# SyncE issues the copies of keys, and six of twelve first gathers are asked for later

## The chip, the core and the metric

The kernel runs on one core of a Trainium2 chip. The core has five engines that run side by side and wait for one another by semaphores: TensorE (PE, matmuls; its weight loads are shown apart as PEld), VectorE (DVE), ScalarE (ACT), GpSimd (POOL) and SyncE (SP, which computes nothing and issues transfers). ACT, SP and POOL can each issue a DMA transfer from their own queue; 16 DMA engines carry all of them. The metric is the device time of one execution in microseconds (us), lower is better.

## The reference

A token block of 2048 rows of 512 is normalised, and two layers are added to it: attention with 32 query heads of 16 and one shared key and value head, and a mixture of 4096 experts from which each token and head takes two, by two searches of 64 keys each.

```python
x = A_x
xn = _layernorm(x, axis=-1)
return x + _A_ref(xn, A_wq, A_wk, A_wv, A_wo) + _B_ref(xn, B_w_q, B_k1, B_k2, B_u, B_v)

# _A_ref: q = xn @ wq (32 heads of 16), k = xn @ wk, v = xn @ wv (one head)
p = softmax(q k^T * 16 ** -0.5);  out = (p v) @ wo
# _B_ref, for each token and head: the two best of 64 keys on either half of a query,
#   the two best of their four sums, gates g by a softmax over the two
act = gelu(xn . u[top_e]);  out = sum of g * act * v[top_e]
```

## The kernel before

Tokens stand in 16 tiles of 128, four tiles to a group, four groups. The program has two parts.

The start (lines 1179 to 1229) makes what attention needs, group by group. `norm_group` normalises four tiles (DVE, with one square root on ACT). `transpose_group` turns them on PE into `ptr` and splits each into a high and a low part `xt` or `xtt`, the high part by a cast on ACT (L181), the low one on DVE (L182); the later groups are stored to HBM (`dxt`, L185, four transfers of 512 KB). `project_kv` makes the keys and values of the group (`pkv`, L198), copies them out on ACT (`kv`, L201), splits them on DVE (`kh`) and then writes the 16 rows of keys six times into the tile `kaug`, which the attention scores read: L207, L208 and L209, once for each of two bases, 32 KB each. In the kernel before, ACT issues these six transfers. `project_q` makes the queries: four steps of 12 matmuls (`pq`, L227); each step is cast on ACT (`qt`, L231), its low part is made on DVE (L232), its square on ACT (`qsq`, L234) goes through one matmul on PE (`pqs`, L235), and SP stores both parts (`dqh`, `dql`, L237 and L238, 256 KB each). `qt` has four buffers, two for each step, so the third step's cast waits until the first step's stores have landed.

Between the second and the third group, the start also makes the expert search of the first chunk of heads: `pw` and `pwt` (L485, L492), 48 matmuls `psc` (L530), the two best by DVE (L543, L545) and from them row numbers. With these, twelve indirect gathers on POOL (L960, `g`, 512 KB each) fetch expert rows; `gathers(NGB)` in line 1217 asks for all twelve. The pool `g` has twelve buffers, so no further gather can start before the main part has used one.

At the end of the start `guard` (L251 to L265) reduces the largest norms to one flag; every engine reads it and branches.

The main part (from line 1230) is written out in a fixed order for all engines: attention in 512 steps (`sc` L325, exponential on ACT L328, `pv` L339), with the expert work laid in between.

The order of the start is made otherwise. A scheduler takes the instructions in the order of the code as a priority, weighs its own costs for each, and fixes for each engine a list that the engine then works off strictly in that order. So a change of the engine of one transfer can move instructions on all engines up to the flag, and none after it. The transfers that SP and ACT issue take eight semaphores (`DMAHW0` to `DMAHW7`) in turn; each issue waits until the transfer that had the same semaphore before, eight back, has landed. The gathers have eight of their own (`DMASW`).

Of the kernel before, what the change touches and what calls it, by code (L numbers as in the profile page):

```python
# [40 lines left out]
NGB = 12  # L41
# [14 lines left out]
def tile_kernel(ctx, tc, x, wq, wkv, wo, wqT, kT, uv, ub, vb, out):  # L56
    nc = tc.nc
# [11 lines left out]
    raw = lambda ap: ap.bitcast(F32)  # L69
# [23 lines left out]
    kaug = const.tile([P, S], F32R, name="kaug")  # L93
# [34 lines left out]
    def load_x(t, first):  # L128
        if first:
            xa = big.tile([P, 2, D], F32, name="xa", tag="xa", bufs=TPH)  # L130
            ACC[t], XN[t] = xa[:, 0, :], xa[:, 1, :]
            xs = xa[:, 0, :]
        else:
            if t % 2 == 0:
                if t // GT == 2:
                    XP[0] = big.tile([P, 2, D], F32, name="xp", tag="wk", bufs=NWK)
                else:
                    XP[0] = start.tile([P, 2, D], F32, name="xp", bufs=2)
            xs = XP[0][:, t % 2, :]
            XN[t] = xs  # L140
        nc.sync.dma_start(xs, x[t * P:(t + 1) * P, :])
        return xs
# [27 lines left out]
    def transpose_group(g):  # L170
        first = g < 1
        XT[g] = []
        for k in range(KC):
            if first:
                xt = big.tile([P, 2, 512], F32R, name="xt", tag="xt", bufs=4)
            else:
                xt = start.tile([P, 2, 512], F32R, name="xtt", tag="xtt", bufs=6)
            p = xtile("ptr")
            for j in range(GT):
                nc.tensor.transpose(p[:, j * P:(j + 1) * P], XN[g * GT + j][:, k * P:(k + 1) * P], ident)  # L180
            nc.scalar.copy(xt[:, 0, :], p)  # L181
            nc.vector.tensor_tensor(out=xt[:, 1, :], in0=p, in1=xt[:, 0, :], op=OP.subtract)  # L182
            XT[g].append(xt)
            if not first:
                nc.sync.dma_start(d_xt[g - 1][k], raw(xt[:]))  # L185
# [6 lines left out]
    def project_kv(g):  # L192
        p = stile("pkv")[:, 0, :]
        n = 0
        for k in range(KC):
            for a, b in TERMS:
                w = (wkv_h, wkv_l)[a]
                nc.tensor.matmul(p[:32, :], w[:, k, :], XT[g][k][:, b, :], start=n == 0, stop=n == 11)  # L198
                n += 1
        kv = big.tile([32, 512], F32, name="kv", tag="wk", bufs=NWK)  # L200
        nc.scalar.copy(kv, p[:32, :])  # L201
        kh = big.tile([32, 2, 512], F32R, name="kh", tag="wk", bufs=NWK)
        nc.vector.tensor_copy(kh[:, 0, :], kv)
        nc.vector.tensor_tensor(out=kh[:, 1, :], in0=kv, in1=kh[:, 0, :], op=OP.subtract)
        c = slice(g * 512, (g + 1) * 512)
        for base in (0, 64):
            nc.scalar.dma_start(raw(kaug[base:base + 16, c]), raw(kh[:16, 0, :]))  # L207
            nc.scalar.dma_start(raw(kaug[base + 16:base + 32, c]), raw(kh[:16, 1, :]))  # L208
            nc.scalar.dma_start(raw(kaug[base + 32:base + 48, c]), raw(kh[:16, 0, :]))  # L209
        sq = start.tile([16, 512], BF16, name="ksq", tag="sq", bufs=2)  # L210
        nc.vector.tensor_mul(sq, kv[:16, :], kv[:16, :])
        nc.tensor.matmul(ksq_p[32 * g:32 * g + 32, :], blk[:16, 0:1].to_broadcast([16, 32]), sq,
                         start=True, stop=True)
        pt = xtile("pv_t")
        for c in range(GT):
            nc.tensor.transpose(pt[:, 32 * c:32 * c + 32], kv[:, c * P:(c + 1) * P], ident[:32, :32])
        nc.vector.tensor_copy(vaug[:, GT * g:GT * g + GT, :DH],
                              pt[:, :P].rearrange("p (c n) -> p c n", n=32)[:, :, DH:])

    def project_q(g, wqs):  # L220
        pq = xtile("pqs")
        for r in range(KC):
            p = stile("pq")[:, 0, :]
            n = 0
            for k in range(KC):
                for a, b in TERMS:
                    nc.tensor.matmul(p, wqs[k][:, a, r * P:(r + 1) * P], XT[g][k][:, b, :],  # L227
                                     start=n == 0, stop=n == 11)
                    n += 1
            q = [start.tile([P, 512], F32R, name="qt", tag="qt", bufs=4) for _ in range(2)]  # L230
            nc.scalar.copy(q[0], p)  # L231
            nc.vector.tensor_tensor(out=q[1], in0=p, in1=q[0], op=OP.subtract)  # L232
            sq = start.tile([P, 512], BF16, name="qsq", tag="sq", bufs=2)
            nc.scalar.activation(sq, p, AF.Square)  # L234
            nc.tensor.matmul(pq[32 * r:32 * r + 32, :], blk, sq, start=True, stop=True)  # L235
            c = slice(g * 512, (g + 1) * 512)
            nc.sync.dma_start(d_qh[r * P:(r + 1) * P, c], raw(q[0][:]))  # L237
            nc.sync.dma_start(d_ql[r * P:(r + 1) * P, c], raw(q[1][:]))  # L238
        nc.vector.reduce_max(qmax[:, g:g + 1], pq, axis=AX.X)
# [713 lines left out]
    def gather(m):  # L953
        ph, c, ti, s = slots[m]
        if s == 0:
            run_scores(key=(ph, c, ti))
            if ph and c == 0:
                load_phase2_tile(TPH * ph + ti)
        gt = gtile()
        nc.gpsimd.indirect_dma_start(  # L960
            out=gt, out_offset=None, in_=uv,
            in_offset=bass.IndirectOffsetOnAxis(ap=IDX[ph, c, ti][:, s:s + 1], axis=0))
        UV[m] = gt
# [50 lines left out]
    def gathers(most):  # L1014
        while g_next[0] < NSL and g_next[0] < a_next[0] + NGB - lent[0] and most > 0:
            gather(g_next[0])
            g_next[0] += 1
            most -= 1
# [24 lines left out]
    def run(fns):  # L1043
        todo = fns[:]
        fns.clear()
        for fn in todo:
            fn()
# [147 lines left out]
    for i in range(2):  # L1195
        for k in range(2):
            w = start.tile([P, 2, 512], F32R, name="wqs", tag="wqs", bufs=4)
            nc.scalar.copy(w[:, 0, :], wraws[i][:, k, :])
            nc.gpsimd.tensor_tensor(out=w[:, 1, :], in0=wraws[i][:, k, :], in1=w[:, 0, :], op=OP.subtract)
            wqs.append(w)  # L1200
    project_kv(0)
    norm_group(1, xs[1])
    project_q(0, wqs)
    transpose_group(1)
    project_kv(1)
    for base in (48, 112):
        nc.scalar.dma_start(raw(kaug[base:base + 2, :]).rearrange("r (i n) -> r i n", n=512),
# [5 lines left out]
    project_q(1, wqs)  # L1213
    transpose_group(2)
    project_kv(2)
    xs.append([load_x(3 * GT + j, False) for j in range(GT)])
    gathers(NGB)
    project_q(2, wqs)
    norm_group(3, xs[3])
    transpose_group(3)  # L1220
    project_kv(3)
    project_q(3, wqs)
    run(STORES)
    start_stack.close()
# [90 lines left out]
def build(nc, tc, args):  # L1315
    tile_kernel(tc, *args)
# [33 lines left out]
```

## Time and profile before

| what | us |
|---|---|
| three runs, median (lowest, highest) | 1978.41 (1978.28, 1985.47) |
| profiled execution | 1969.9 |
| its span, first to last instruction | 1968.2 |
| PE busy | 1871.4 |
| DVE busy | 1678.5 |
| ACT busy | 1291.5 |
| POOL busy | 563.0 |
| the flag is written on DVE at | 131.2 |
| first matmul of attention (`sc`) at | 147.9 |

The start is the first 131 us of the span, the branch and the first weights take the next 16, and the rest is the main part. All times of single instructions below are counted from the start of the span. In a row of the timeline stand the start, the time from start to end of the whole row, the engine, the line, the operation and, in brackets, how long the engine was idle before it and what it waited for. `ACTq` and `SPq` are an engine's queue, which issues transfers.

### The profile page before, as it was taken

How to read it: one execution, taken by the hardware profiler on the slowest of the kernel's cores; microseconds unless marked ns; L12 is line 12 of the kernel's file. 1: busy time of each engine (PE TensorE's matmuls, PEld its weight loads, DVE VectorE, ACT ScalarE, POOL GpSimd, SP SyncE). 2: the span in 40 equal slices, each digit the busy share in tenths (PEclk: the TensorE clock that was granted, in tenths of full speed). 3: DMA queues.
4: the chain of work that ended last, by engine and by line, in shares of the span. 5: the costliest groups of instructions: out<-in, count | busy, mean ns of one | idle time of the engine just before them, and what ended most of it. 6: DMA issues, size and time to landing. Idle time of an engine off the chain costs nothing.

```text
span 1968.2 us, 34715 instructions
## 1 busy us (share of the span) xinstructions
PE 1871.4 (95%) x10990; PEld 993.5 (50%) x10990; DVE 1678.5 (85%) x6713; ACT 1291.5 (66%) x1801; POOL 563.0 (29%) x540
## 2 busy tenths in 40 slices
PE   6879999999998998999999999999989899999997
PEld 3544444555554543555555445555545454555552
DVE  6527888999998975899999789999989878899993
ACT  3326666655556885778777555655568877788773
POOL 2202223321222222344344232222222224343420
PEclk9989999999998899999999999999988899999998
DMA  7756879887764886798889987777647878788872
GB/s 281 280 198 232 294 264 304 288 294 240 252 216 137 215 233 213 236 289 290 266 290 312 345 291 255 266 264 236 205 130 210 255 230 285 246 295 267 270 250 80
DMA packets 238041, 492.16 MB, mean 250 GB/s; under 512 B 93204, under 2 KB 93204, under 8 KB 237852
## 3 DMA queue, kind: packets, MB, share of 16 engines
q0 software_dynamic: 73728, 268.47, 41.2%
q1 hardware_dynamic: 162120, 219.82, 34.1%
q10 hardware_dynamic: 2004, 1.61, 0.3%
q8 instruction: 88, 1.44, 0.3%
q14 instruction: 101, 0.83, 0.1%
HBM read 428.46 MB, written 56.07 MB: 246 GB/s over the span
## 4 chain that ended last, share of the span: by engine, by line
PE 65%; DVE 19%; DMA 5%; ACT 2%; issue 2%; SPq 0%; ACTq 0%; DVEq 0%
PE pv L339 19%; PE sc L325 13%; PE psc L530 9%; PE pout L846 9%; PE pact L722 9%; DVE i L545 5%; DVE m L543 3%; DVE xa L1007 3%; PE pg L804 3%; DVE g L972 3%; ACT pt L328 2%; PE pwo L432 2%; PE pw L485 1%; DMA dg<-gst 1%; DMA wqt<-in_wqT_dram 1%
## 5 line engine op out<-in xcount | busy, mean ns | idle before, releaser
L328 ACT ACTIVATE pt<-sc 128x1024 f32<-128x1024 f32 x1024 | 993.1, 1025 | 460.6 <-PE sc L325 459.5
L960 POOL DMA_INDIRECT g<-in_uv_dram,idx x512 | 550.1, 1074 | 1342.9 <-DVE xa L1007 703.0
L339 PE MATMUL pv<-pt,vaug 128*32 128x512 f32 x4096 | 517.1, 623 | 0.0
L325 PE MATMUL sc<-qa,kaug 64*128 64x512 f32 x2048 | 387.8, 454 | 21.0 <-ACT pt L328 20.6
L530 PE MATMUL psc<-wk,xt 128*128 128x512 f32 x1536 | 388.5, 400 | 2.4 <-DVE wk L495 2.0
L1007 DVE SCALAR_TENSOR_TENSOR xa<-g,w,xa 128x512 f32<-128x512 f32 x512 | 371.2, 744 | 0.0
L972 DVE CUSTOM_DVE_ANT_0 g<-g,xa 128x512 f32<-128x512 f32 x512 | 335.5, 680 | 1.0 <-DMA g<-in_uv_dram,idx 0.9
L530 PEld LDWEIGHTS psc<-wk,xt 128*128 128x128 f32 x1536 | 277.6, 188 | 106.1 <-issue 37.4
L325 PEld LDWEIGHTS sc<-qa,kaug 64*128 64x128 f32 x2048 | 156.8, 186 | 342.7 <-ACT pt L328 233.8
L339 PEld LDWEIGHTS pv<-pt,vaug 128*32 128x32 f32 x4096 | 109.8, 112 | 258.6 <-issue 257.0
L545 DVE FIND_INDEX8 i<-m,psc 128x8 uint32<-128x64 f32 x1024 | 206.3, 220 | 0.0
L846 PE MATMUL pout<-wk,wd 128*128 128x512 f32 x768 | 195.4, 402 | 2.8 <-DVE wd L904 2.7
L722 PE MATMUL pact<-xt,wk 128*128 128x512 f32 x768 | 195.9, 400 | 1.4 <-DVE i L545 1.4
L846 PEld LDWEIGHTS pout<-wk,wd 128*128 128x128 f32 x768 | 140.6, 188 | 50.8 <-DVE act L972 5.1
L722 PEld LDWEIGHTS pact<-xt,wk 128*128 128x128 f32 x768 | 139.4, 188 | 50.2 <-issue 17.9
L543 DVE MAX8 m<-psc 128x8 f32<-128x64 f32 x1024 | 145.9, 213 | 17.5 <-PE psc L530 16.8
L995 DVE SCALAR_TENSOR_TENSOR w<-gth,ga 128x4 f32<-128x4 f32 x128 | 20.2, 158 | 84.9 <-ACT gth L988 84.6
L687 DVE TENSOR_TENSOR wk<-rw,wk 128x512 fp32r<-128x512 f32 x128 | 85.0, 682 | 6.6 <-ACT wk L686 6.6
L849 DVE TENSOR_TENSOR da<-da,pout 128x512 f32<-128x512 f32 x128 | 82.8, 678 | 4.0 <-PE pout L846 3.6
L770 DVE TENSOR_TENSOR oh<-oh 128x2048 f16<-128x2048 f16 x64 | 78.0, 1218 | 0.0
L686 ACT CAST wk<-rw 128x512 fp32r<-128x512 f32 x128 | 73.9, 629 | 2.9 <-DMA rw<-in_ub_dram 2.9
L804 PEld LDWEIGHTS <-oh 128*128 128x128 f16 x1024 | 68.3, 165 | 14.4 <-issue 6.8
(155 smaller groups left out, 1337.2 us busy)
## 6 DMA issues: line engine op xcount, KB each, us to landing
wk<-dw SPq DMA_DIRECT2D x96, 512.0 KB
wqt<-in_wqT_dram SPq DMA_DIRECT2D x32, 512.0 KB
dw<-wk SPq DMA_DIRECT2D x32, 512.0 KB
rw<-in_ub_dram SPq DMA_DIRECT2D x64, 256.0 KB
rw<-in_vb_dram SPq DMA_DIRECT2D x64, 256.0 KB
gy<-dg SPq DMA_DIRECT2D x64, 256.0 KB
dg<-gst SPq DMA_DIRECT2D x30, 512.0 KB
qa<-dqh SPq DMA_DIRECT2D x128, 64.0 KB
```

The lines of the kernel that those rows point to most:

```text
L325: nc.tensor.matmul(p[:, b, :], kaug[o:o + 64, kc * P:(kc + 1) * P], QA[u][o:o + 64, i, :], start=True, stop=True)
L328: nc.scalar.activation(pt, p, AF.Exp, scale=SCALE)
L339: nc.tensor.matmul(PV[u][32 * j:32 * j + 32, :], vaug[:, kc, :], pt[:, b, :], start=kc == 0, stop=kc == 15)
L530: nc.tensor.matmul(p, XT[g][k][:, a, j * P:(j + 1) * P], WC[n_][k][:, bb, :], start=n == 0, stop=n == 11)
L543: nc.vector.max(m8[:, jb, s, :], p[:, s * E:(s + 1) * E])
L545: nc.vector.max_index(i8[:, jb, s, :], m8[:, jb, s, :], p[:, s * E:(s + 1) * E])
L722: nc.tensor.matmul(p, us[:, a, k * P:(k + 1) * P], XT[DG][k][:, c, :], start=n == 0, stop=n == 11)
L804: nc.tensor.matmul(p[:, i * NB:(i + 1) * NB], oa[:, :, i], ob[:, :, i], start=True, stop=True)
L846: nc.tensor.matmul(p, wd[0][:, a, j * P:(j + 1) * P], vs[:, c, :], start=n == 0, stop=n == 5)
L960: nc.gpsimd.indirect_dma_start(out=gt, out_offset=None, in_=uv, in_offset=bass.IndirectOffsetOnAxis(ap=IDX[ph, c, ti][:, s:s + 1], axis=0))
L972: nc.vector.tensor_tensor_reduce(u, u, XN[TPH * ph + ti], scale=1.0, scalar=0.0, op0=OP.mult, op1=OP.add, accum_out=a[:, i:i + 1])
L1007: nc.vector.scalar_tensor_tensor(acc, v, w[:, i:i + 1], acc, op0=OP.mult, op1=OP.add)
```

## The change

Two things are changed in the code. The six copies of keys of each group are issued by SP instead of ACT (24 transfers in all), and line 1217's twelve gathers are asked for in two halves: six where they stood, six after `project_kv(3)`, ahead of `project_q(3)`.

```diff
         for base in (0, 64):
-            nc.scalar.dma_start(raw(kaug[base:base + 16, c]), raw(kh[:16, 0, :]))
-            nc.scalar.dma_start(raw(kaug[base + 16:base + 32, c]), raw(kh[:16, 1, :]))
-            nc.scalar.dma_start(raw(kaug[base + 32:base + 48, c]), raw(kh[:16, 0, :]))
+            nc.sync.dma_start(raw(kaug[base:base + 16, c]), raw(kh[:16, 0, :]))
+            nc.sync.dma_start(raw(kaug[base + 16:base + 32, c]), raw(kh[:16, 1, :]))
+            nc.sync.dma_start(raw(kaug[base + 32:base + 48, c]), raw(kh[:16, 0, :]))
...
     xs.append([load_x(3 * GT + j, False) for j in range(GT)])
-    gathers(NGB)
+    gathers(NGB // 2)
     project_q(2, wqs)
     norm_group(3, xs[3])
     transpose_group(3)
     project_kv(3)
+    gathers(NGB // 2)
     project_q(3, wqs)
     run(STORES)
```

POOL's own list stays what it was: the twelve gathers follow each other, with nothing between them, ahead of the flag. What moves are the lists of PE, DVE, ACT and SP up to the flag. On PE, 73 of the `pq` matmuls stood ahead of the 48 `psc` matmuls, now 57: sixteen of the second group's queries go behind them.

The first place is ACT in the third group, from the last transposes to the queries. Before (in brackets the semaphores that each row waits for):

```order
L181 CAST xtt<-ptr 128x512 [waits DMAHW7_49,PE_49]
L201 COPY kv<-pkv 32x512 [waits PE_49]
L207 DMA kaug<-kh 16x512 [waits DMAHW0_49,DVE_49]
L209 DMA kaug<-kh 16x512 [waits DMAHW1_49]
L208 DMA kaug<-kh 16x512 [waits DMAHW2_49,DVE_49]
L207 DMA kaug<-kh 16x512 [waits DMAHW3_49]
L208 DMA kaug<-kh 16x512 [waits DMAHW4_49]
L209 DMA kaug<-kh 16x512 [waits DMAHW5_49]
L231 CAST qt<-pq 128x512 [waits PE_49,Activation_49] x2
L234 ACTIVATE qsq<-pq 128x512 [waits DVE_49] x2
```

The same place on ACT with the change:

```order
L181 CAST xtt<-ptr 128x512 [waits DMAHW2_49,PE_49]
L201 COPY kv<-pkv 32x512 [waits PE_49]
L231 CAST qt<-pq 128x512 [waits DMAHW3_49,PE_49,Activation_49]
L234 ACTIVATE qsq<-pq 128x512 [waits DVE_49]
L231 CAST qt<-pq 128x512 [waits DMAHW6_49,PE_49]
L234 ACTIVATE qsq<-pq 128x512 [waits DVE_49]
```

The six transfers are gone from ACT's list, and the queries' casts follow the keys at once.

The second place is SP in the same group, from the stores of the transposed tokens to the queries. Before:

```order
L185 DMA dxt_0_76<-xtt 128x1024 [waits DMAHW4_49,DVE_49]
L185 DMA dxt_1_77<-xtt 128x1024 [waits DMAHW5_49,DVE_49]
L185 DMA dxt_2_78<-xtt 128x1024 [waits DMAHW6_49,DVE_49]
L185 DMA dxt_3_79<-xtt 128x1024 [waits DMAHW7_49,DVE_49]
L237 DMA dqh<-qt 128x512 [waits DMAHW6_49,Activation_49]
L238 DMA dql<-qt 128x512 [waits DMAHW7_49,DVE_49]
```

The same place on SP with the change:

```order
L185 DMA dxt_0_76<-xtt 128x1024 [waits DMAHW0_49,DVE_49]
L185 DMA dxt_1_77<-xtt 128x1024 [waits DMAHW1_49,DVE_49]
L185 DMA dxt_2_78<-xtt 128x1024 [waits DMAHW2_49,DVE_49]
L185 DMA dxt_3_79<-xtt 128x1024 [waits DMAHW3_49,DVE_49]
L207 DMA kaug<-kh 16x512 [waits DMAHW4_49,DVE_49]
L208 DMA kaug<-kh 16x512 [waits DMAHW5_49,DVE_49]
L209 DMA kaug<-kh 16x512 [waits DMAHW6_49]
L207 DMA kaug<-kh 16x512 [waits DMAHW7_49]
L208 DMA kaug<-kh 16x512 [waits DMAHW0_49]
L209 DMA kaug<-kh 16x512 [waits DMAHW1_49]
L237 DMA dqh<-qt 128x512 [waits DMAHW2_49,Activation_49]
L238 DMA dql<-qt 128x512 [waits DMAHW3_49,DVE_49]
```

The six copies now stand between the stores of the tokens and those of the queries. The fifth and sixth copy wait for the first two `dxt` stores to land, the first step's `dqh` and `dql` for the last two.

The third place is ACT right behind the branch, at the first exponentials of attention. Before:

```order
L486 COPY wt<-pw 128x512 x4
L494 CAST wk<-pwt 128x512 x4
L328 ACTIVATE pt<-sc 128x1024 x8
L486 COPY wt<-pw 128x512
L328 ACTIVATE pt<-sc 128x1024 x2
```

With the change:

```order
L486 COPY wt<-pw 128x512 x4
L494 CAST wk<-pwt 128x512 x4
L328 ACT_TABLE_LOAD
L328 ACTIVATE pt<-sc 128x1024 x8
L486 COPY wt<-pw 128x512
L328 ACTIVATE pt<-sc 128x1024 x2
```

A load of ACT's function table has come in. The fourth group's square root (L153) now stands behind the expert search's exponential (L582) and no longer ahead of it, so it loads the table of the root, and the first exponential of attention loads that of the exponential again: two loads more than before.

## The prediction

> **What bounds the kernel now.** I read the page's busy times and its chain first, then the windows by stage, the waits of the start, and last the timeline there, because nothing behind the flag changes its order.
>
> ```profile
> PE 1871.4 (95%) x10990; PEld 993.5 (50%) x10990; DVE 1678.5 (85%) x6713; ACT 1291.5 (66%) x1801; POOL 563.0 (29%) x540
> PE 65%; DVE 19%; DMA 5%; ACT 2%; issue 2%; SPq 0%; ACTq 0%; DVEq 0%
> 0.00:131.24 131.24, 98.30 (x422) 64.37 (x422) 75.14 (x247) 40.41 (x72) 24.83 (x40) 0.96 0.74 267
> 131.24:160.00 28.76, 18.40 (x86) 6.77 (x90) 6.03 (x17) 13.24 (x18) 0.00 (x0) 0.81 0.55 182
> 160.00:1968.00 1808.00, 1754.74 (x10490) 922.40 (x10481) 1597.32 (x6449) 1237.81 (x1712) 538.17 (x500) 0.98 0.76 250
> ```
>
> The first two lines are the page's parts on busy time and on the chain; the windows give length, busy us of PE, PEld, DVE, ACT and POOL, the PE clock granted, the DMA share and GB/s. PE is the engine that paces the whole, 1754.7 of 1808 us in the main part. In the start it works 98.3 of 131.2 us. The main part is one fixed list per engine and waits for no clock time, so what the start gains or loses reaches the end one for one; I take that share as 1.
>
> Where PE stands in the start, the waits from 24 to 131 us say:
>
> ```profile
> PE pqs L235 <- ACT qsq L234: 14.2, 7, 6.3
> ACT qt L231 <- DMA kaug<-kh: 14.1, 2, 9.8
> ```
>
> PE waited 14.2 us in seven places for ACT's squares, once for 6.3 us; ACT in turn stood 14.1 us in two places behind the copies of keys. The timeline shows the copies on ACT's queue (first and last of the six of a group), what ACT did next, and PE beside it:
>
> ```profile
> 24.90 0.59 ACTq L207 DMA_DIRECT2D kaug<-kh  x1
> 28.56 0.94 ACTq L209 DMA_DIRECT2D kaug<-kh  x1
> 30.29 0.38 PE L235 MATMUL pqs<-qsq,blk 128*32 128x512 bf16 x1 [1.62 <-ACT qsq L234]
> 33.98 0.38 PE L235 MATMUL pqs<-qsq,blk 128*32 128x512 bf16 x1 [1.49 <-ACT qsq L234]
> 46.57 0.53 ACTq L207 DMA_DIRECT2D kaug<-kh  x1
> 50.05 0.53 ACTq L209 DMA_DIRECT2D kaug<-kh  x1
> 58.60 11.04 PE L530 MATMUL psc<-wk,xt 128*128 128x512 f32 x48
> 69.89 5.51 PE L227 MATMUL pq<-xtt,wqs 128*128 128x512 f32 x23
> 84.16 0.52 ACTq L207 DMA_DIRECT2D kaug<-kh  x1
> 91.53 1.83 ACTq L209 DMA_DIRECT2D kaug<-kh  x1
> 93.46 1.07 ACT L231 CAST qt<-pq 128x512 fp32r<-128x512 f32 x2 [9.77 <-DMA kaug<-kh]
> 95.45 0.59 PE L235 MATMUL pqs<-qsq,blk 128*32 128x512 bf16 x1 [6.28 <-ACT qsq L234]
> 112.31 0.52 ACTq L207 DMA_DIRECT2D kaug<-kh  x1
> 115.43 0.60 ACTq L209 DMA_DIRECT2D kaug<-kh  x1
> 119.00 0.38 PE L235 MATMUL pqs<-qsq,blk 128*32 128x512 bf16 x1 [1.23 <-ACT qsq L234]
> ```
>
> Six copies hold ACT's queue 4.6, 4.0, 9.2 and 3.7 us in the four groups. In the second group PE had other work; in the third nothing was left, and it stood 6.28 us. After that stall the clock was low:
>
> ```profile
> 94.00:96.00 2.00, 0.55 (x2) 0.04 (x1) 1.29 (x2) 1.72 (x4) 0.00 (x0) 0.54 1.02 391
> 96.00:98.00 2.00, 2.00 (x5) 0.92 (x5) 0.00 (x0) 0.00 (x0) 0.00 (x0) 0.50 1.04 367
> 98.00:100.00 2.00, 2.00 (x6) 1.52 (x6) 0.00 (x0) 0.00 (x0) 0.00 (x0) 0.50 1.04 418
> 100.00:102.00 2.00, 2.00 (x8) 1.64 (x7) 0.00 (x0) 0.17 (x1) 0.00 (x0) 0.75 1.01 404
> ```
>
> **The change, part by part.**
>
> *ACT loses the copies, third group.* The 6.28 us of idle time go. With them goes the slow clock behind: PE busy times what the clock lacked, 0.55 x 0.46 + 2 x 0.50 + 2 x 0.50 + 2 x 0.25, or 2.8 us by the four windows above. Together -9.1. The cover of this is DMA work, taken up below.
>
> *First and second group.* 1.62 + 1.49 = 3.1 us of idle PE hang on ACT's queue in the first group; in the second PE's idle time is nil. The new list puts sixteen transposes in a row on PE with four casts behind them on ACT, so part comes back. Ends 0 and -3.1; I take -2, nearer to the row that is removed.
>
> *Fourth group.* The 1.23 us at 119.00 are of the same kind, and the queue holds only 3.7 us there: -1.2, ends 0 and -1.2.
>
> *The gathers.* POOL's list is the same, so the second six go out right behind the first six as before: 0. They start when the search is ready, and that is earlier: sixteen `pq` matmuls (23 take 5.51 us, so 0.24 each) no longer stand ahead of the search, 3.8 us, and the 2 us above. The matmuls themselves are not saved.
>
> *SP gains the copies: the new wait.* The gathers fill the DMA engines:
>
> ```profile
> 74.63 1.11 POOL L960 DMA_INDIRECT g<-in_uv_dram,idx  x1 [59.24 <-DVE e L598]
> 78.64 3.89 SPq L185 DMA_DIRECT2D dxt<-xtt  x4
> 74.00:102.00 28.00, 20.27 (x82) 13.06 (x81) 10.60 (x34) 8.33 (x15) 11.90 (x12) 0.88 0.97 366
> q0 software_dynamic: 1710, 6.23, 59.4%
> q1 hardware_dynamic: 1507, 3.81, 34.6%
> g<-in_uv_dram,idx POOLq DMA_INDIRECT x12, 12.2
> ```
>
> From 74 to 102 us the DMA engines are 97% busy at 366 GB/s (the queue rows are of that window: packets, MB, share). A gather takes 12.2 us from issue to landing there, and SP issues four `dxt` stores in 3.9 us. In the new SP list the third group's first query stores stand behind four `dxt` stores and six copies, the last of which wait for two `dxt` to land, and `dql` for the fourth. The third step's cast on ACT needs those stores landed, and PE's next `pqs` needs that cast. By bytes: twelve gathers (6.3 MB), the second group's seven later stores (7 x 0.26), four `dxt` (2.1), copies and loads of 0.3 MB make 10.5 MB; at 390 GB/s, the middle of the fine windows, 27 us. The search began at 58.60 and the gathers 16.0 us later; now it begins near 53, the gathers near 69, and the stores land near 69 + 27 + 2 = 98 (2 us for the last store's own way, an estimate); cast, low part and square take 2.0 us, as from 93.46 to 95.45 above, so `pqs` can go near 100. PE's work from the search to that point is 11 us of `psc`, 87 `pq` at 0.24 (20.9), and some 8 us of 24 transposes, 12 `pkv` and small matmuls, with 2.7 us of short waits such as these of the third group:
>
> ```profile
> 77.25 0.41 PE L198 MATMUL pkv<-xtt,wkv_h 128*32 128x512 f32 x1 [0.50 <-ACT xtt L181]
> 78.62 0.38 PE L235 MATMUL pqs<-qsq,blk 128*32 128x512 bf16 x1 [0.95 <-ACT qsq L234]
> ```
>
> That is 42.7 us, so PE arrives near 95.7: a stall of about 4.3 us. Whether the clock drops after that lies between two rows: after 6.28 us it fell, after 1.62 it did not; I add 1.7, some half of the 2.8. Together +6.0. The ends are 0 (the stores land before PE arrives) and +9.1 (the old stall, whole, in a new place). SP's own issue time is no cost: it waits here anyway.
>
> *Two table loads.* One is on the path: the first exponential follows the scores at once, and PE waits for it.
>
> ```profile
> 74.11 0.60 ACT L234 ACTIVATE qsq<-pq 128x512 bf16<-128x512 f32 x1 [0.76 <-DVE qt L232]
> 74.73 1.28 ACT L582 ACT_TABLE_LOAD   x1
> 76.02 0.22 ACT L582 ACTIVATE ex<-mx 128x16 f32<-128x16 f32 x1
> 148.62 5.69 ACT L328 ACTIVATE pt<-sc 128x1024 f32<-128x1024 f32 x6 [0.91 <-PE sc L325]
> 152.44 0.79 PE sc L325 x2
> ```
>
> The load takes 1.28 us, with 0.02 us before and 0.01 behind it: +1.3. The other, for the fourth group's root, falls into a stretch in which ACT mostly waits; 0, at most 1.3. The Trainium skill (ScalarE: Activation LUTs, What ACT_TABLE_LOAD costs) gives a load 1283 ns and, on top, a drain of some 1380 ns, 2.66 us for each switch. The trace agrees with the first figure and shows no drain. By that rule the sum below would be some 1.4 us nearer to zero.
>
> Sum: -9.1 - 2.0 - 1.2 + 6.0 + 1.3 = -5.0 us. The terms come from an execution of 1969.9 us (span 1968.2 and 1.7 around it), which would become 1964.9; that execution is 8.5 us, 0.4%, below the median of the runs. Measured against 1978.4 I predict 1973.4 us.
>
> **The rivals.**
>
> *The stall does not come back.* If the third group's stores land before PE needs them, the +6.0 falls away: -11.0, 1967.4. For it: in the new list PE has 42 us of work in front. Against it: 97% busy DMA engines and a list in which `dql` waits for all four `dxt`.
>
> *Nothing gained.* The stall moves whole from ACT's queue to SP's, at -9.1 + 9.1 + 1.3: 1979.7, or 1976.5 where the small terms of -3.2 still come. For it: the same transfers cross the same full engines. The Trainium skill says so as a rule (DMA: Bandwidth & Descriptors, Issuing engines are not separate DMA queues): transfers from any engine run on the same 16 DMA engines, and a second issuing engine saves only the time of issue, usually small. Its first half agrees with the full windows here; "small" does not, since 9.2 us of issue time stood on ACT in the third group. That ACT's casts no longer stand behind it is against this rival.
>
> *Slower.* The place is SP's list in the third group: one queue in order, at most eight transfers open, and PE's queries hang on its stores. The price is what the stores come later than I reckon. To lose 0.5% (10 us) against the other terms of -11.0 it needs a stall and slow clock of 21 us, 18 of them stall, so stores that land near 112 instead of 98: 10.5 MB in 41 us, 256 GB/s. For it: SP's queue had 34.6% of the engines against the gathers' 59.4%, and a queue that waits eight back can leave its share unused. Against it: the fine windows are full at 367 to 418 GB/s whoever issues.
>
> **How the numbers follow.** About 0.5% is what a measurement of this kernel can tell from no change. Chances: my forecast (1968.5 to 1976.5) 0.52, the stall that does not come back 0.22, nothing gained 0.15, slower 0.11. The bounds of all terms together, -9.1 - 3.1 - 1.2 + 0 + 1.3 = -12.1 and -9.1 + 0 + 0 + 9.1 + 2.6 = +2.6, give 1966.3 to 1981.0; I widen the lower end to 1966 and leave out the slower rival and the fringe of the faster one. Faster by over 0.5% is below 1968.5: most of the first rival, 0.22. Slower by over 0.5%: most of the last, 0.10. Within: 0.68.
>
> **What would show it.** In the profile of the changed kernel: no copies of keys on ACT's queue, and its casts within a microsecond of PE's `pq` in groups one and four; the search near 53 and the first gather near 69 us; a wait of PE for ACT's square in the third group of about 4 us, ACT there waiting for a `dqh` or `dql` store; two more table loads of 1.28 us, one ahead of the first exponential; the flag near 125 us against 131.2, and from there the same length as before but for 1.3 us. The prediction is wrong if that wait is missing, or over 10 us, or if the part behind the flag changes its length by more than 2 us.

## The result, and the profile after

The change makes no difference that can be measured. Over 20 runs of each, the changed kernel takes 1980.43 us in the median (1975.67 to 1996.41) and the kernel before 1980.12 (1967.45 to 1988.99): a ratio of 1.0005 with a 95% interval of 0.9989 to 1.0022. A second set of runs (experiment 1) gives 0.9986 (0.9964 to 1.0008). Forecast were 1973.4 against 1978.4, a ratio of 0.9975.

The page of the changed kernel, on busy time and on the chain, and its windows of the start, the branch and the main part:

```profile
PE 1883.1 (95%) x10990; PEld 995.6 (50%) x10990; DVE 1678.6 (85%) x6713; ACT 1295.1 (65%) x1803; POOL 565.2 (29%) x540
PE 65%; DVE 19%; DMA 4%; ACT 2%; issue 2%; SPq 1%; ACTq 0%; DVEq 0%
0.00:129.80 129.80, 100.00 (x422) 64.52 (x422) 74.50 (x247) 42.55 (x73) 24.46 (x40) 0.94 0.75 270
129.80:160.00 30.20, 20.80 (x94) 7.25 (x94) 6.03 (x18) 15.54 (x20) 0.00 (x0) 0.75 0.53 178
160.00:1979.00 1819.00, 1762.24 (x10478) 923.83 (x10474) 1598.09 (x6449) 1236.96 (x1711) 540.78 (x500) 0.98 0.76 248
```

The start ends at 129.8 us, 1.4 us earlier than before, where 6.2 were forecast. This execution took 1981.3 us and the one shown of before 1969.9, but nearly all of that lies in the main part, whose lists are the same: from the thirteenth gather to the last it took 1756.1 us here and 1743.9 before, and 1760.1 in the second execution below. So the whole says little about a few microseconds, and I read the start by marks in it: the first gather, the flag's first matmul `pm`, and the thirteenth gather, which is the first that the main part issues.

The waits of the changed kernel from 24 us to the flag, which answer to the two rows shown of before:

```profile
PE pqs L235 <- ACT qsq L234: 5.9, 5, 2.0
PE pqs L235 <- issue: 5.3, 2, 3.8
ACT xtt L181 <- remote: 3.9, 1, 3.9
```

No wait for `kaug` is left on ACT, and PE's 14.2 us ahead of `pqs` have become 11.2. The timeline shows where they lie now (PE, POOL, ACT and SP, put together in order of time):

```profile
36.45 1.25 PE L180 MATMUL ptr<-ident,xp 128*128 128x128 f32 x8 [0.96 <-DVE xtt L182]
39.73 0.58 PE L235 MATMUL pqs<-qsq,blk 128*32 128x512 bf16 x1 [2.03 <-ACT qsq L234]
55.35 11.09 PE L530 MATMUL psc<-wk,xt 128*128 128x512 f32 x48
70.75 1.11 POOL L960 DMA_INDIRECT g<-in_uv_dram,idx  x1 [55.98 <-DVE e L598]
78.80 0.38 PE L235 MATMUL pqs<-qsq,blk 128*32 128x512 bf16 x1 [1.56 <-issue]
85.09 0.59 ACT L181 CAST xtt<-ptr 128x512 fp32r<-128x512 f32 x1 [3.86 <-remote]
86.22 0.58 PE L235 MATMUL pqs<-qsq,blk 128*32 128x512 bf16 x1 [3.76 <-issue]
103.78 0.59 ACT L231 CAST qt<-pq 128x512 fp32r<-128x512 f32 x1 [2.84 <-DMA dqh<-qt]
106.61 0.38 PE L235 MATMUL pqs<-qsq,blk 128*32 128x512 bf16 x1 [0.74 <-ACT qsq L234]
117.59 0.38 PE L235 MATMUL pqs<-qsq,blk 128*32 128x512 bf16 x1
128.42 0.59 PE L256 MATMUL pm<-ident,mm 128*1 128x128 f32 x2 [1.07 <-DVE mm L252]
146.08 1.28 ACT L328 ACT_TABLE_LOAD   x1 [0.88 <-PE sc L325]
147.37 5.76 ACT L328 ACTIVATE pt<-sc 128x1024 f32<-128x1024 f32 x6
```

The first group's waits at `pqs` are gone, but a new one of 2.03 us comes at 39.73. The search starts at 55.35 and the gathers at 70.75, 3.9 us earlier than before. Among the gathers PE stands 3.76 us at 86.22, since ACT stood 3.86 us ahead of a cast for which everything in its list was there (the bracket's "remote" names none of this core's engines). The third step's cast waits for a store of queries until 103.78, as forecast, but PE comes late to it and loses only 0.74. The fourth group's 1.23 us are gone (117.59 has no bracket). Behind the flag, the table load stands where it was put, and takes 1.28 us.

### The profile page after: what moved, and what is told of

The parts are those of the page before. It is cut to its first block, busy times and chain, and to the rows that moved or that the text cites. A ratio compares the mean times of both kernels' runs of the same rounds, so it can differ in the third digit from the quotient of the medians.

```text
span 1979.5 us, 34717 instructions
## 1 busy us (share of the span) xinstructions
PE 1883.1 (95%) x10990; PEld 995.6 (50%) x10990; DVE 1678.6 (85%) x6713; ACT 1295.1 (65%) x1803; POOL 565.2 (29%) x540
## 4 chain that ended last, share of the span: by engine, by line
PE 65%; DVE 19%; DMA 4%; ACT 2%; issue 2%; SPq 1%; ACTq 0%; DVEq 0%
PE pv L339 19%; PE sc L325 13%; PE psc L530 9%; PE pact L722 9%; PE pout L846 9%; DVE i L545 5%; DVE m L543 3%; DVE xa L1007 3%; PE pg L804 3%; DVE g L972 3%; ACT pt L328 2%; PE pw L485 1%; PE pwo L432 1%; DMA dg<-gst 1%; DMA dinv<-rc 1%
## 5 line engine op out<-in xcount | busy, mean ns | idle before, releaser
L339 PE MATMUL pv<-pt,vaug 128*32 128x512 f32 x4096 | 524.5, 631 | 0.0
L545 DVE MATCH_VALUE_LOAD i<-m,psc 128x8 f32 x1024 | 81.2, 79 | 0.0
```

Of the source, the lines that this page charges most:

```text
L339: nc.tensor.matmul(PV[u][32 * j:32 * j + 32, :], vaug[:, kc, :], pt[:, b, :], start=kc == 0, stop=kc == 15)
L545: nc.vector.max_index(i8[:, jb, s, :], m8[:, jb, s, :], p[:, s * E:(s + 1) * E])
```

## The experiments

The second edit needs no run of its own: with the gathers asked for in two halves and the copies left on ACT, the instructions stand in the same order as before on all five engines; with the copies on SP and the gathers asked for in one, they stand as in the changed kernel. What follows is therefore about the copies.

In experiments 6 to 10 the lists of PE, ACT and DVE, and SP's transfers, stay in the order of the kernel they start from; in the others the lists change around the edit. This table has their marks (first gather, `pm`, thirteenth gather, in us of the profiled execution) and the ratio of times to the kernel before. The marks are of one execution each, and executions are apart before any list differs: the first `pqs` comes at 29.61 to 30.61 us in the seven that have the list of before up to there, and at 27.86 to 29.20 in the seven that have the changed one. So about 1 us between two marks says nothing.

| kernel | first gather | `pm` | 13th gather | ratio (95%) |
|---|---|---|---|---|
| before | 74.63 | 129.85 | 163.15 | |
| changed | 70.75 | 128.42 | 162.20 | 1.0005 (0.9989 to 1.0022) |
| 1 changed, again | 70.33 | 130.22 | 167.06 | 0.9986 (0.9964 to 1.0008) |
| 2 changed, 24 more on ACT | 70.08 | 129.82 | 166.51 | 1.0004 (0.9979 to 1.0029) |
| 3 SP for the third group only | 74.00 | 127.92 | 160.90 | 0.9979 (0.9953 to 1.0005) |
| 4 SP for the first two groups | 70.29 | 131.50 | 166.58 | 1.0020 (0.9999 to 1.0041) |
| 5 changed, no third copies | 70.70 | 132.11 | 165.43 | |
| 6 changed, gathers held | 107.78 | 125.04 | 163.76 | 0.9997 (0.9969 to 1.0026) |
| 7 before, gathers held | 106.00 | 123.19 | 156.50 | 0.9975 (0.9949 to 1.0001) |
| 7 the same, again | 106.31 | 123.70 | 159.49 | 0.9966 (0.9945 to 0.9988) |
| 8 before, six held | 74.30 | 127.92 | 159.83 | 0.9999 (0.9977 to 1.0022) |
| 9 before, held to third maxima | 101.63 | 127.00 | 160.40 | 0.9964 (0.9941 to 0.9987) |
| 10 before, held to fourth maxima | 122.08 | 122.00 | 165.33 | 0.9994 (0.9964 to 1.0025) |
| 11 changed, no second root | 70.91 | 129.72 | 164.55 | 1.0018 (0.9990 to 1.0046) |

**1. The changed kernel again.** No edit.

> The changed kernel as it is, once more. If the waits between 70 and 107 us belong to the program (lists, stores, gathers), ACT stands idle again for about 3.9 us ahead of the second cast of the third group's transposes, PE for about 3.8 us ahead of the `pqs` behind it, and the flag's `pm` comes within 1.5 us of 128.4. If they are chance, that wait is missing or elsewhere. Ratio to the kernel before within 0.2% of 1.0005.

The wait of ACT at the second cast is missing. In its place stands the wait that was forecast, in the third step of the third group. Timeline, and windows (length, busy PE, PEld, DVE, ACT, POOL, clock, DMA share, GB/s):

```profile
104.21 0.58 ACT L231 CAST qt<-pq 128x512 fp32r<-128x512 f32 x1 [9.39 <-DMA dqh<-qt]
106.21 0.58 PE L235 MATMUL pqs<-qsq,blk 128*32 128x512 bf16 x1 [6.43 <-ACT qsq L234]
130.22 0.58 PE L256 MATMUL pm<-ident,mm 128*1 128x128 f32 x2 [1.06 <-DVE mm L252]
70.30:104.10 33.80, 26.70 (x119) 17.99 (x119) 14.33 (x39) 11.05 (x19) 11.55 (x12) 0.97 1.02 364
106.00:108.00 2.00, 1.79 (x7) 1.07 (x6) 1.42 (x3) 1.13 (x3) 0.00 (x0) 0.50 0.84 312
108.00:110.00 2.00, 2.00 (x7) 0.67 (x4) 0.69 (x1) 1.08 (x2) 0.00 (x0) 0.50 1.00 390
110.00:112.00 2.00, 2.00 (x7) 1.18 (x7) 0.95 (x2) 0.59 (x1) 0.00 (x0) 0.50 1.02 406
q1 hardware_dynamic: 2846, 6.08, 53.1%
q0 software_dynamic: 1728, 6.29, 48.6%
```

So the 3.86 us were chance, and no part of the explanation. Without them PE reaches the third step's `pqs` early, at 99.8, and stands 6.43 us; behind it the clock is half for 5.8 us of busy PE, another 2.9 us. `pm` comes at 130.22, later than before. The last two rows are the DMA queues from 70 to 104 us: 6.3 MB of gathers and 6.1 MB of SP's transfers.

**2. Twenty-four more instructions on ACT, early.** The only transfer of instructions between 70 and 100 us fell into ACT's 3.86 us, so I moved it.

```diff
-    norm_group(0, xs[0])
+    norm_group(0, xs[0]); pd = start.tile([2, 24], F32, name="pd"); [nc.scalar.copy(pd[:, i:i + 1], kTs[:2, 0, i:i + 1]) for i in range(24)]
```

> The changed kernel with 24 tiny copies on ACT at about 4 to 7 us, where it is idle; the lists are the same otherwise. They move the places in ACT's instruction stream at which its next block of instructions is fetched, 24 instructions earlier, out of the stretch in which the gathers fill the DMA engines. If ACT's idle 3.9 us ahead of the second cast at 85.1 us (nothing in the program is missing there, and the one instruction transfer of the stretch is at 82.1) is such a fetch, that wait goes, and `pm` comes 2 to 5 us earlier. If it is a wait for a store or for PE, it stays, and `pm` is within 1 us.

The transfer did move: the 8 KB that started at 82.1 us start at 40.4 here, and none is left among the gathers. It is ACT's fetch. The wait at the second cast is missing too, but it is missing in experiment 1 with the fetch in its old place (81.7 us). Whether the fetch stopped ACT in the first execution stays open. `pm`, at 129.82, is near experiment 1 and neither value expected; here, too, the forecast wait is back, PE's longest of all:

```profile
106.01 0.59 PE L235 MATMUL pqs<-qsq,blk 128*32 128x512 bf16 x1 [7.36 <-ACT qsq L234]
```

**3. SP for the third group only.**

```diff
-            nc.scalar.dma_start(raw(kaug[base:base + 16, c]), raw(kh[:16, 0, :]))
+            (nc.sync if g == 2 else nc.scalar).dma_start(raw(kaug[base:base + 16, c]), raw(kh[:16, 0, :]))
...
```

> The kernel before with only the third group's six copies on SyncE; up to the third group all lists are those of before, so the search and the gathers start as before (58.6 and 74.6 us). If the wait moves whole from ACT's queue to SyncE's list (query stores behind copies, copies behind `dxt` stores that wait among the gathers), PE's 6.3 us at 95.5 go and a wait of 5 to 8 us comes back ahead of a later `pqs` of the same group, ACT standing there for a store of queries that lands near 105; `pm` is then within 2 us of 129.85. If the third group's gain is real and was lost in the changed kernel only since its gathers start 4 us earlier, the later wait is under 2 us and `pm` comes at 121 to 125.

```profile
99.80 0.58 ACT L231 CAST qt<-pq 128x512 fp32r<-128x512 f32 x1 [8.65 <-DMA dqh<-qt]
103.08 0.58 PE L235 MATMUL pqs<-qsq,blk 128*32 128x512 bf16 x1 [6.99 <-ACT qsq L234]
127.92 0.59 PE L256 MATMUL pm<-ident,mm 128*1 128x128 f32 x2 [1.07 <-DVE mm L252]
```

With search and gathers where they were before, the wait of 6.28 us at 95.45 still comes back as 6.99 at 103.08. The third group's copies on SP are worth 1.9 us at `pm`, no more, and 0.7 of that is there already when the search starts (57.92 against 58.60), ahead of the first difference between the lists. That the gathers start earlier in the changed kernel is not needed to lose the gain.

**4. SP for the first two groups only.**

```diff
-            nc.scalar.dma_start(raw(kaug[base:base + 16, c]), raw(kh[:16, 0, :]))
+            (nc.sync if g < 2 else nc.scalar).dma_start(raw(kaug[base:base + 16, c]), raw(kh[:16, 0, :]))
...
```

> The kernel before with only the first two groups' copies on SyncE; the third and fourth group's stay on ACT. If what these two groups gain is lost again before the search (ACT's casts wait for transposes and for stores of queries, the clock falls to half), PE ends the second group's `pkv` within 1 us of before, the search starts some 3 us earlier only because sixteen `pq` go behind it, ACT's copies of the third group still take about 9 us among the gathers, PE waits there for 5 us or more, and `pm` is at 129 to 131. If the gain of 2 to 3 us is real, `pm` comes at 126.5 to 128.

```profile
40.43 0.58 PE L235 MATMUL pqs<-qsq,blk 128*32 128x512 bf16 x1 [2.03 <-ACT qsq L234]
54.90 11.07 PE L530 MATMUL psc<-wk,xt 128*128 128x512 f32 x48
70.63 0.38 PE L235 MATMUL pqs<-qsq,blk 128*32 128x512 bf16 x1 [1.22 <-ACT qsq L234]
97.52 0.59 PE L235 MATMUL pqs<-qsq,blk 128*32 128x512 bf16 x1 [5.74 <-ACT qsq L234]
131.50 0.38 PE L256 MATMUL pm<-ident,mm 128*1 128x128 f32 x2 [1.07 <-DVE mm L252]
```

These groups do not gain 2 us, they lose 1.7: `pm` at 131.50 against 129.85. Sixteen transposes now stand in a row on PE and wait for DVE (0.97 us), then `pqs` waits 2.03 us for a square whose cast stands on ACT behind the four casts of these transposes, and the clock falls to half. That is a part of it. The search starts 3.7 us earlier than before, where the sixteen `pq` alone would give 3.8 and this execution began 0.6 us earlier (first transpose at 12.90 against 13.52): 0.7 us are lost up to there. The rest is lost behind the search, where the second group's queries now stand and `pqs` has a new wait of 1.22 us (70.63). The third group's six copies, on ACT's queue as before, took 8.7 us.

**5. No copies in the third group.**

```diff
-        for base in (0, 64):
+        for base in (0, 64) * (g != 2):
```

> The changed kernel without the third group's six copies (its keys stay zero, the scores are not the reference's; the time of everything else is). In the unchanged list they make the first store of queries leave SyncE at 96.4 us and land at 104.1. If what counts is only the bytes of the gathers, it still lands at 103 or later and PE waits for 5 us or more. If the copies are what holds the stores back (each waits until the transfer eight before it has landed), the store leaves near 90, lands at 98 to 101 behind the last `dxt` store, and PE waits for 1 to 4 us.

SP's store, ACT's cast behind its landing, and PE:

```profile
89.36 0.32 SPq L237 DMA_DIRECT2D dqh<-qt  x1
101.99 0.58 ACT L231 CAST qt<-pq 128x512 fp32r<-128x512 f32 x1 [8.00 <-DMA dqh<-qt]
104.60 0.59 PE L235 MATMUL pqs<-qsq,blk 128*32 128x512 bf16 x1 [7.20 <-ACT qsq L234]
```

Between the two expectations. The store leaves SP 7.0 us earlier than in experiment 1, yet lands only 2.2 us earlier, and PE, which is earlier as well, waits 7.20 us. So of what holds the stores back the copies are 2.2 us; the rest is, as experiment 6 bears out, the data of the gathers and of the `dxt` stores ahead of them. `pm` comes no earlier for it: the clock stays at half over 8.1 us of busy PE behind the wait, against 5.8 in experiment 1.

**6. The changed kernel with all gathers held back.** A copy of one column on POOL reads the last value tile, so the first gather cannot go before the fourth group's values stand; all twelve are asked for behind `project_kv(3)`.

```diff
-        gt = gtile()
+        gt = gtile(); [nc.gpsimd.tensor_copy(gt[:, 0:1], vaug[:, NT - 1, 0:1]) for _ in [0] if m == 0]
...
```

> The changed kernel with all twelve gathers held back until the fourth group's values stand: a one-column copy on POOL ahead of the first gather reads the last value tile. The lists of PE, ACT, DVE and SP are the same. If the gathers' full DMA engines cause the waits in the second and third group, PE's idle rows of 1.2, 1.6 and 3.8 us between 70 and 87 go, with the half clock behind, query stores land in 2 to 5 us instead of 6 to 8, and `pm` comes at 118 to 121 us instead of 128.4; the whole is then some 5 us faster if the late gathers (about 110 to 140 us) hold nothing up, and the same or slower if the first dots or the loads of `wqt` behind the flag wait for them. If the waits come from the order of the lists, `pm` stays at 126 or later.

```profile
74.00:102.00 28.00, 26.19 (x120) 17.54 (x120) 14.25 (x33) 12.47 (x22) 0.00 (x0) 1.00 0.59 219
99.67 0.38 PE L235 MATMUL pqs<-qsq,blk 128*32 128x512 bf16 x1 [0.74 <-ACT qsq L234]
123.39 0.59 PE L235 MATMUL pqs<-qsq,blk 128*32 128x512 bf16 x1 [3.64 <-ACT qsq L234]
125.04 0.58 PE L256 MATMUL pm<-ident,mm 128*1 128x128 f32 x2 [1.07 <-DVE mm L252]
133.94 3.32 PE L485 MATMUL pw<-wqt,kTs 128*64 128x512 f32 x8 [8.31 <-SPq L264]
```

In the window from 74 to 102 us the DMA engines are now 59% busy instead of 97, PE works 26.2 of 28 us instead of 20.3 in the kernel before, and the clock granted is 1.00. The third group's wait is gone. `pm` comes 5.2 us earlier than in experiment 1, though not at the 118 to 121 expected, since the gathers now make the fourth group wait (3.64 us); and the branch takes PE 8.3 us instead of 5.3, waiting for SP (why SP is later there, no run shows). At the thirteenth gather, 163.76, the kernel lies between the two executions of the changed one (162.20 and 167.06).

**7. The kernel before with all gathers held back.** The same edit, with the copies on ACT, in two sets of runs.

> The kernel before, copies on ACT's queue, with all twelve gathers held back in the same way. If the copies cost ACT 9.2 us in the third group only because the DMA engines were full, they now take 0.5 to 0.6 us each, 3.7 us, PE's wait of 6.3 us shrinks to 1.6 or less, and `pm` comes at 120 to 122 us instead of 129.85; SP instead of ACT is then worth 1 to 2 us. If ACT's queue is what costs whatever the DMA engines do, a wait of 3 us or more stays and `pm` is at 125 or later.

First and last copy of the third group on ACT, and PE there, at the flag and at the branch:

```profile
83.66 0.52 ACTq L207 DMA_DIRECT2D kaug<-kh  x1
...
86.78 0.60 ACTq L209 DMA_DIRECT2D kaug<-kh  x1
89.89 0.38 PE L235 MATMUL pqs<-qsq,blk 128*32 128x512 bf16 x1 [1.23 <-ACT qsq L234]
123.19 0.59 PE L256 MATMUL pm<-ident,mm 128*1 128x128 f32 x2 [1.07 <-DVE mm L252]
131.56 3.52 PE L485 MATMUL pw<-wqt,kTs 128*64 128x512 f32 x8 [7.79 <-PEq L264]
```

This settles the cause. Without the gathers beside them, the six copies cost ACT 3.7 us instead of 9.2, PE waits 1.23 us instead of 6.28, and `pm` comes 6.7 us earlier than in the kernel before. ACT's queue was slow because the gathers filled the DMA engines. `pm` at 123.19 is later than the 120 to 122 expected, and the 1 to 2 us expected from SP did not come: with the gathers out of the way `pm` is at 123.19 and 123.70 with the copies on ACT, at 125.04 with SP. The whole was 0.25% shorter, with an interval that just reaches 1.0001.

> The kernel before with all twelve gathers held back until the fourth group's values stand, once more, for its time. Its first 160 us were 6.6 us shorter, 0.34%: ratio 0.994 to 0.9995 if the main part neither gives this back nor adds to it.

The second set gives 0.9966 (0.9945 to 0.9988), within what was expected.

**8. The kernel before with six gathers held back.** What the change's second edit says in words: the gathers asked for in two halves, and the seventh made to wait.

```diff
-        gt = gtile()
+        gt = gtile(); [nc.gpsimd.tensor_copy(gt[:, 0:1], vaug[:, NT - 1, 0:1]) for _ in [0] if m == 6]
...
```

> The kernel before with the second six of the gathers held back until the fourth group's values stand (what the change's second edit says in words, and does not do). If the full DMA engines are the cost in the third group, half of it goes: PE's wait of 6.3 us falls to 2 to 4 and `pm` comes at 124 to 127 (123.2 with all twelve held back, 129.85 with none). Behind the flag fewer transfers are open than with twelve, so PE's wait at the branch is nearer to 5.4 us than to 7.8, and the thirteenth gather comes at 156 to 160. If only the first six matter, `pm` stays at 129 or later.

PE's wait in the third group falls to 3.94 us, and `pm` comes at 127.92, less of a gain than expected; the wait at the branch (5.27 us) and the thirteenth gather (159.83) are as expected. The ratio, 0.9999, shows nothing.

**9 and 10. Held back to another point.** As experiment 7, but the copy reads the third group's largest squares (`qmax[:, 2:3]`), or the fourth's.

> The kernel before with all twelve gathers held back until the third group's largest squares stand (about 97 us); the lists of PE, ACT and SP are those of before. If the gathers cost what they collide with, the third group's wait of 6.3 us is 1.6 or less as with the later hold, the fourth group's stores and copies are slower (PE waits there for 3 to 6 us in all), and the branch costs PE 5.4 to 6.5 us instead of 7.8, since fewer transfers are open there: `pm` at 122 to 126, the thirteenth gather at 154.5 to 158.

> The kernel before with all twelve gathers held back until the fourth group's largest squares stand (about 121 us). The whole start is then free of them: the fourth group's waits stay at 1.2, 1.4 and 2.0 us and `pm` comes at 122 to 123. What is open is the stretch behind it: if the gathers then hold up the loads of `wqt` (4 x 512 KB behind the branch), PE waits for them for 5 us or more and the thirteenth gather comes at 158 or later; if not, at 153 to 156.

Held to the third group's maxima, the gathers start at 101.6 us. The third group's wait is 1.23 us, the fourth group waits longer than expected (1.34, 3.58 and 2.53), and the branch is back at 5.3 us: 0.9964 (0.9941 to 0.9987), as good as experiment 7, and with it faster than the kernel before. Against the changed kernel, whose own ratios are 1.0005 and 0.9986, neither was measured side by side. `pm` at 127.00 and the thirteenth gather at 160.40 came later than expected. Held to the fourth group's maxima, the start is free of them and `pm` comes at 122.00, but then PE waits for weights behind the branch (the chain there stands 12.36 us at the loads of `wqt`, against 5.98 in the kernel before), and all is given back:

```profile
139.08 1.97 PE L485 MATMUL pw<-wqt,kTs 128*64 128x512 f32 x4 [6.93 <-issue]
```

**11. No second root on ACT.**

```diff
-        nc.scalar.activation(sd, v, AF.Sqrt)
         y = start.tile([P, GT], F32, name="rs", bufs=2)
-        nc.vector.reciprocal(y, sd)
-
+        if g < 3: nc.scalar.activation(sd, v, AF.Sqrt); nc.vector.reciprocal(y, sd)
+        else: nc.vector.tensor_scalar(y, v, -4000.0, 30.0, op0=OP.mult, op1=OP.add)
+        for _ in range(3 * (g == 3)): nc.vector.tensor_mul(sd, y, y); nc.vector.tensor_mul(sd, sd, v); nc.vector.tensor_scalar(sd, sd, -0.5, 1.5, op0=OP.mult, op1=OP.add); nc.vector.tensor_mul(y, y, sd)
```

> The changed kernel with the fourth group's root by four Newton steps on VectorE, so that ACT needs neither the second table of roots nor to load the table of exponentials again. If a load costs its own 1.28 us and nothing more, the first exponential starts 0.7 us behind the first `sc` instead of 1.97, and `pm` moves by less than 1 us. If a load also drains the engine, the first exponentials gain 2.5 us or more.

The first `sc` and the first exponential:

```profile
148.30 0.73 PE L325 MATMUL sc<-qa,kaug 64*128 64x512 f32 x4
148.99 5.68 ACT L328 ACTIVATE pt<-sc 128x1024 f32<-128x1024 f32 x6 [0.90 <-PE sc L325]
```

The exponential follows 0.69 us behind the first `sc`; with the load it was 1.97 (145.40 to 147.37). The load costs 1.28 us and nothing more. The wait for a store of queries is in this run too: PE stands 6.30 us at 106.22, here at a transpose.

## Why the prediction was wrong

The measured time lies in the range, and most of the chance stood on no change. The forecast itself, 5 us faster, failed; the rival "nothing gained" (1976.5 to 1979.7) is what happened: 1.0005 times the 1978.4 that it starts from is 1979.4. Two terms of the sum failed, the new wait, which was sized 3.3 us too small, and the first and second group, which was 3.7 us off and had the wrong sign. By its own steps:

- *Third group, -9.1.* Right. The wait of 6.28 us ahead of the third group's first `pqs`, and the slow clock behind it, are gone in every execution with these copies on SP.
- *The new wait, +6.0.* The place and the chain were right: PE at `pqs`, ACT's third cast, a store of queries behind SP's copies. The size was wrong. Stores that were to land near 98 us landed near 104.1 (experiment 1). I counted 10.5 MB at 390 GB/s, 27 us; from 70.3 to 104.1 us there went 364 GB/s, or 12.3 MB in 33.8 us. SP's part was 6.1 MB where I had 4.2: I left out the `wqt` loads issued just ahead of the gathers and the third group's own first stores, and took the rate of the four full windows for the whole. PE was there at 99.8 and not 95.7, which made up for some of it. The wait was 6.43 us and the slow clock 2.9, together +9.3: the upper end, +9.1, was the value.
- *First and second group, -2.0.* Wrong in sign, and outside the ends of 0 and -3.1. By experiment 4 it is +1.7 at `pm`. I had bounded it by the waits that are removed and asked only whether they come back. But the list that has sixteen transposes in a row waits for the low parts on DVE and for a cast behind four others on ACT; with the wait of 2.03 us the clock went down in all seven executions with this list, which it had not done with the removed waits of 1.62 and 1.49; and the queries that went behind the search wait there anew.
- *Fourth group, -1.2.* Right: no wait at 117.59.
- *The gathers, 0, but earlier.* Right in kind: the split changes nothing, and the gathers start at 70.75 where I had 69.
- *Table loads, +1.3 and 0.* The first is right: 1.97 - 0.69 = 1.28 us, by experiment 11; that the other costs nothing is not shown by itself. The Trainium skill (ScalarE: Activation LUTs, What ACT_TABLE_LOAD costs) adds a drain of some 1380 ns to each switch; the trace disagrees, there is none here.

Summed anew: -9.1 + 1.7 - 1.2 + 9.3 + 1.3 = +2.0 us, 0.1%, which no measurement here can tell from nothing. The sum is good to some 2 us: the third group's two terms make +0.2 in it, and -1.9 at `pm` in experiment 3. The sign of being wrong by the part behind the flag could not be read, since with the same lists that part differs by over 10 us from one execution to the next. The first execution of the changed kernel, 1.4 us better than before at `pm`, had its waits elsewhere: 3.76 us at 86.22 made PE late for the other.

What the forecast lacked is that both queues were slow for one reason. Experiments 6 and 7 show it: hold the gathers back, and the third group's wait goes whichever queue issues the copies. The Trainium skill (DMA: Bandwidth & Descriptors, Issuing engines are not separate DMA queues) says that transfers of all issuing engines share the same DMA engines. The runs agree, with a wait of 6.28 us on one queue against 6.30 to 7.36 on the other (experiments 1, 2, 3 and 11). I cited it in the prediction and gave its case a chance of 0.15, since 9.2 us of ACT's time looked like a price of the queue; it was a price of the full engines, 3.7 us without them.

## What to carry to other kernels

When a queue is slow, look first at what fills the DMA engines beside it: if they are full, as they were here, another queue can get the same wait at the next instruction that needs a landing. Move the bulk transfer, not the small ones; here the kernel before with its twelve gathers later, by one tiny instruction that waits, is some 0.3% faster where they start at 102 to 106 us, and not measurably with six of them held or with a start at 122; the changed kernel gains nothing measurable with a start at 108. And price a wait by the bytes that lie ahead of it, all queues counted, at the rate of the whole stretch.

## What the runs showed of the hardware

- The third group's six copies held ACT's queue for 3.7 us with the DMA engines 58% busy from 74 to 102 us (experiment 7), and for 9.2 us with them 97% busy (the kernel before); on SP, among the gathers, they took 7.3 us (experiment 1). Where the time lies differs from run to run, and not by the queue alone: in the kernel before five of the six issues on ACT take 1.18 to 2.53 us each, while in experiment 4, also on ACT among the gathers, each takes 0.51 to 0.60 us and the time lies between them, as on SP in experiment 1.
- In the changed kernel the clock of PE fell to half at about 39 us, within the second of two gaps of 0.96 and 2.03 us that lay 1.25 us apart, and stayed there until after 45 us (the rows from 42 to 44 us also have 0.50):

```profile
38.00:40.00 2.00, 0.27 (x1) 0.00 (x0) 2.00 (x4) 1.49 (x3) 0.00 (x0) 0.71 0.44 173
40.00:42.00 2.00, 2.00 (x6) 0.73 (x6) 0.24 (x1) 0.60 (x1) 0.00 (x0) 0.50 1.03 389
44.00:46.00 2.00, 2.00 (x7) 0.94 (x6) 0.28 (x1) 0.00 (x0) 0.00 (x0) 0.59 0.92 367
```

  The Trainium skill (TensorE: Matmul & The Clock Gate, HAM oscillation — how this bites in real kernels) warns of idle gaps over some 3.4 us. No gap here was that long, and the clock fell all the same: 0.96 us of idle time and, by the 0.71 of the first row, some 1.1 us more, with 1.25 us of work between them, were enough. Nor does the length of one gap decide: behind a wait of 2.03 us in the fourth group `pqs` took 0.38 us, its time at full clock, in experiment 4 (130.05) and 0.55 us in the kernel before (128.23).
- The DMA queues of the profile include one of kind "instruction" with transfers of 8 KB. Twenty-five instructions more on ACT (24 copies and a table load) moved one of them from 82.1 to 40.4 us, so these are ACT's fetches, and they go through the same DMA engines as the kernel's transfers.
